# An attention block on one core: late constants among GpSimd's planned work, other PSUM banks for the opening's norms, J1 tiles taken at their addition

## The chip, the core and the metric

The kernel runs on one core of a Trainium2 chip. A core has five engines that run their own instruction streams side by side: TensorE (PE, matrix products into PSUM), VectorE (DVE), ScalarE (ACT, table functions such as the exponential), GpSimd (POOL) and SyncE (SP, which here only issues DMAs). They meet through semaphores. PSUM has eight banks of 128 partitions x 2 KB.

The metric is the time of one execution on the device in microseconds (us), the median over several runs. Before the change it is 359.07 us, the median of 3 runs (359.01 to 359.48).

## The reference

One multi-head attention block: x is 1 x 2048 x 448 in bf16, 16 heads of width 28.

```python
B, S, D = x.shape
H = 16
Dh = D // H
qkv = (x @ wqkv).reshape(B, S, 3, H, Dh).transpose(2, 0, 3, 1, 4)
q, k, v = qkv[0], qkv[1], qkv[2]
scores = jnp.einsum("bhqd,bhkd->bhqk", q, k) * (Dh ** -0.5)
p = softmax(scores, axis=-1)
o = jnp.einsum("bhqk,bhkd->bhqd", p, v)
return o.transpose(0, 2, 1, 3).reshape(B, S, D) @ wo
```

Softmax does not change when one number is taken from all scores of a query. The kernel takes an upper bound on them, made of the norm of the query and the largest norm of the keys.

## The kernel before

**Tiling.** The heads stand in 4 groups of 4 (each padded to 32 rows, so that a group fills 128 partitions), the queries in 4 columns of 512, the keys in 16 tiles of 128. A *set* is one group with one column of queries: 16 sets, in the order ORDER, almost one after the other. Within a set there are 4 x 16 score tiles of 128 keys x 512 queries, one for each head and key tile.

**Two ways to exponentiate.** Most score tiles go in pairs through PSUM tiles a0 and a1 (two banks each) to ScalarE, which takes the exponential of 128 x 1024 numbers at once into a tile `pt` (L1001, `do_exp`). The others go through banks d0 and d1, and now and then m, to VectorE (L1016, `do_a`): it adds a bias, clamps at zero and writes 16-bit integers, whose bits read as bf16 are about 2 to the power of the score. Four such tiles make a *chain*, one tile `I` of 128 x 2048 16-bit integers. To come nearer to the true power, the chain is used three times: as it is, with 43 added to the integers (SHIFT[1], tile J1) and with 85 added (SHIFT[2], tile J2), multiplied with V, V x WT[1] and V x WT[2] (VS or VW in the trace). The additions are VectorE's (L1114, `do_add`; both J1 and J2 appear as J). In sets in the middle, a chain that begins while at least FAR2 = 36 tiles of its set remain doesn't get a J2 from VectorE. There GpSimd issues a DMA that adds a constant tile `shift2` into the chain itself, once the plain chain has been read by PE (`in_place`, L1066, issue at L1074). This is called the in-place line here.

**PE's products.** PE makes scores (L798, into a, d or m), sums the weighted values into bank o (L1176, `do_pv`; four heads side by side, one such group of four matmuls is a *wave*), and in between the projections of later groups (L341 through `mm_proj`, L348 through `quarters`) in bank m. Bank m also takes the output projection. Where PE would idle it multiplies zeros (L830 and `quarters` of `zero`).

**Order.** All of it is a hand-made plan. `plan` runs a model of the five engines in which each operation (class `Op`) has a duration, needs, gives, a priority (a smaller number goes first) and perhaps a PSUM bank to acquire and release; `evt`, `free` and `res` hold the times of events, engines and banks. The plan is made dry with 24 seeds that shake some choices (NSEED), and the shortest is then emitted as instructions. So a change in one rule can alter the order on all engines from there on. `port=True` marks operations that the plan never lets run on GpSimd beside a VectorE operation of the same mark; `after_shared` (L350) adds a semaphore by which a GpSimd operation stays behind the VectorE operation that the plan placed ahead of it. Nothing makes VectorE wait for GpSimd in return. What lies ahead of `plan` (L178 to L261) is not planned: it is a fixed stream on each engine, and the plan only assumes that GpSimd is free from 25.6 us on (L277). GpSimd's fixed stream clears V's tiles (L245, L246), issues 14 DMAs that put offset rows into the QP tiles (L231), then fills `shift2` (L257), copies the identity to fp32 (`identf`, L258, read by the closing transposes at L1428) and makes a small selector (L259, L260).

**The opening.** x's first block is transposed by PE, the other three by DMA (L176). Then come the keys of group 0 in four blocks (`k_first`, L419): product K, its square on ScalarE (L367), the norm of each head's rows by a product with a block of ones (`norm`, L452) into the bank `nbank`, the largest norm on VectorE (`red`, L457, tile kp). After the fourth, `root` (L461, L463) makes the keys' bound. The first query column does the same (`q_job`, `qn_first`, L527 to L550): product, square, norm (L530), root (L534), and the product of both roots, `su` (L539), which the first scores need. Banks are handed on: an operation that acquires a bank waits until its last reader has released it.

**Chains and buffers.** `d_more` starts a chain when `dve_ok` (L840) allows: tile I from six buffers (NCH), tile J1 from five (NJ), both taken at the start of the chain (L892, L895); `j1_free` (L1042) holds back the start of a chain until the J1 of five chains ago has been read. J2 is taken at its addition, from three buffers (L1112, `add_ok`). The rules with FAR and LASTFAR (`far_chain`, `accumulate`) never apply, since a set has 64 tiles and FAR is 99.

**The end.** After the last set, VectorE copies o, PE makes reciprocals' transposes (L1422, L1428), and the output projection of the last column is completed in banks d0, d1, m and one of the a tiles. Parts of it that need only earlier groups (`early_jobs`, `filler`) are placed ahead, as banks come free; those left over stand directly ahead of the last groups (L1437). Two casts on VectorE and two on ScalarE (L1440, L1442) and three DMAs end it.

Of the kernel before, what the change touches and what calls it, by code (L numbers as in the profile page):

```python
# [8 lines left out]
ACT = mybir.ActivationFunctionType  # L9
ALU = mybir.AluOpType  # L10
# [43 lines left out]
def kernel(  # L54
# [7 lines left out]
    nc = tc.nc  # L62
# [31 lines left out]
    NJ = 5  # L94
    FAR = 99
# [5 lines left out]
    LASTFAR = 99  # L101
# [154 lines left out]
    shift2 = const.tile([P, HG * QW], I16, name="shift2")  # L256
    nc.gpsimd.memset(shift2[:].bitcast(I32), SHIFT[2] * 65537)  # L257
    nc.gpsimd.tensor_copy(out=identf[:], in_=ident[:])  # L258
# [5 lines left out]
    def plan(nc, tc, psum, big, wk, dram, seed, dry):  # L264
# [443 lines left out]

        for gg in range(G):
            add("POOL", 0.5, lambda gg=gg: clear_wo(gg), need=[("QA", 0, CL)], gives=[("WZ", gg)], pri=95, port=True)  # L710
# [6 lines left out]
        k_first(1, "a1", "a0", "ACT", "ACT", 3.05, late=("ksq", 0, NQC - 1))  # L717
        k_first(2, "d0", "o", "ACT", "ACT", 3.1, late=("ksq", 0, NQC - 1))
        k_first(3, "d1", "a0", "DVE", "ACT", 3.2, late=("QA", 0, 0))
        q_job(0, 0, "m", QPRI, split=1)  # L720
        qn_first("o", 3.15)
# [47 lines left out]
        chain = {"cur": None, "all": [], "J2": [], "dma": 0.0}  # L769
# [70 lines left out]
        def dve_ok(t, k):  # L840
            if chain["cur"] is None and len(chain["all"]) >= NCH:
                old = chain["all"][-NCH]
                if not j1_free() or not used_up(old, 0) or any(a[0] is old for a in adds) or old["acc"] is None or old["acc"] > t:
                    return False
# [35 lines left out]
        def d_more(s, t, acting):  # L880
            got, taken = [], []
            for b in d_banks(t):
# [183 lines left out]
        def in_place(ch, m):  # L1066
# [3 lines left out]
            if used_up(ch, 0):  # L1070
                evt[("PV0", n)] = (free["PE"], "PE")

            def emit():
                after_shared(nc.gpsimd.dma_start(out=ch["I"][:, w], in_=shift2[:, w], accum_op=ALU.add))  # L1074

            def landed(end):
                at = landing(end)
                for q in range(m):
                    pending.append({"step": ch["steps"][q], "k": 2, "ap": ch["I"][:, q * QW:(q + 1) * QW].bitcast(BF16),
                                    "ready": at, "pt": None, "ch": ch})  # L1080

            add("POOL", 0.88, emit, need=[("line1", n), ("PV0", n)], gives=[("own", n)], pri=9, port=True)
            ops["POOL"][-1].after = landed

        def accumulate(ch, m):
            w = slice(0, m * QW)
            ch["acc"] = None

            def emit():
                after_shared(nc.gpsimd.dma_start(out=ch[1][:, w], in_=ch["I"][:, w], accum_op=ALU.add))  # L1090

            def landed(end):
# [400 lines left out]
```

## Time and profile before

| what | us |
|---|---|
| median of 3 runs | 359.07 |
| span of the profiled execution, first to last instruction | 358.24 |
| time of the profiled execution | 360.29 |
| first exponential begins (L1001) | 17.27 |
| last exponential begins | 348.04 |
| VectorE idle ahead of the closing copies (L1417) | 6.16 |
| POOL busy in the whole span | 115.3 |

The granted clock of TensorE is 1.00 throughout. A group in the page names a line, an engine and an operation, then what is written and read, how often, its busy time and mean duration, and the idle time of the engine just before it with what ended it. A timeline line gives start, duration, engine, line and operation. A matmul or an exponential that is pipelined behind the one ahead of it is recorded with a duration that overlaps, so steps between starts tell more than durations do. Where the page says `shift`, it is `shift2`; buffer numbers are left out.

### The profile page before, as it was taken

Reading aid. Unit: us, or ns where it says so; the run is one execution under the profiler, and the core shown is the slowest. Engines: PE = TensorE matmul, PEld = TensorE weight load, DVE = VectorE, ACT = ScalarE, POOL = GpSimd, SP = SyncE. Lnnn points to the kernel's source line nnn. Section 1 sums busy time; section 2 is a strip of 40 time slices with the busy share of each in tenths; the row PEclk is TensorE's granted clock in tenths of the full one; section 3 lists DMA queues with packets and bytes.
Section 4 is the critical chain, followed back from the end, with each engine's and each line's share of the span. In section 5 each row is a group of like instructions: output and inputs, shape, how many; then the busy total and the mean of one; then the engine's idle time right before and its main releaser. Section 6 shows DMA issues by size and latency. Waiting matters only on the chain.

```text
span 358.2 us, 11057 instructions
## 1 busy us (share of the span) xinstructions
PE 338.0 (94%) x4474; PEld 110.3 (31%) x4474; DVE 329.4 (92%) x616; ACT 338.1 (94%) x370; POOL 115.3 (32%) x164
## 2 busy tenths in 40 slices
PE   8999999999999999999989999988899899999994
PEld 4333233332234332332222222222222322222232
DVE  7789989999999899998999999999999999999933
ACT  2689999999999999999999999999999999999991
POOL 8971252413503043432223535121414131130110
PEclk9999999999999999999999999999999999999999
DMA  9430146551746437094393916464585929395211
GB/s 208 105 97 15 25 95 131 119 112 36 147 98 120 91 61 150 10 191 89 86 186 77 193 34 136 94 139 102 104 165 97 198 62 203 90 185 120 66 33 54
DMA packets 29463, 38.73 MB, mean 108 GB/s; under 512 B 15108, under 2 KB 21092, under 8 KB 29412
## 3 DMA queue, kind: packets, MB, share of 16 engines
q0 software_dynamic: 7648, 26.25, 38.5%
q1 hardware_dynamic: 20516, 11.22, 12.2%
q8 instruction: 35, 0.57, 0.7%
q10 hardware_dynamic: 1248, 0.55, 0.6%
q14 instruction: 16, 0.13, 0.1%
HBM read 6.20 MB, written 1.96 MB: 23 GB/s over the span
## 4 chain that ended last, share of the span: by engine, by line
PE 45%; ACT 37%; issue 7%; DVE 6%; DMA 3%; POOL 0%; SPq 0%; POOLq 0%; ACTq 0%; DVEq 0%
ACT pt L1001 37%; PE a L798 17%; PE o L1176 13%; PE m L341 5%; PE m L348 5%; DVE I L1016 3%; DMA scr<-rec 2%; PE o L696 1%; DVE J L1114 1%; DVE kp L457 1%; DMA rr<-scr 1%; PE d L348 1%; PE d L798 1%; PE a L341 1%; DVE V L612 0%
## 5 line engine op out<-in xcount | busy, mean ns | idle before, releaser
L1001 ACT ACTIVATE pt<-a 128x1024 bf16<-128x1024 f32 x358 | 329.5, 1167 | 3.2 <-PE d L798 1.7
L1016 DVE TENSOR_SCALAR I<-d 128x512 int16<-128x512 f32 x278 | 181.4, 680 | 9.2 <-PE d L798 8.6
L798 PE MATMUL a<-QP,KA 32*128 32x512 bf16 (+1 forms) x708 | 138.2, 380 | 11.3 <-ACT pt L1001 10.3
L1176 PE MATMUL o<-pt,V 128*32 128x512 bf16 x716 | 102.7, 383 | 0.0
L798 PE MATMUL d<-QP,KA 32*128 32x512 bf16 x275 | 95.4, 384 | 0.8 <-DVE I L1016 0.8
L798 PEld LDWEIGHTS <-KA 32*128 32x128 bf16 (+1 forms) x1035 | 48.6, 91 | 145.4 <-issue 143.7
L1074 POOL DMA_DIRECT2D I<-shift x50 | 44.0, 941 | 99.9 <-PE o L1176 28.4
L1114 DVE TENSOR_SCALAR J<-I 128x2048 int16<-128x2048 int16 x104 | 72.9, 709 | 0.7
L1176 PE MATMUL o<-I,V 128*32 128x512 bf16 x308 | 60.0, 385 | 0.0
L1176 PE MATMUL o<-J,VS 128*32 128x512 bf16 x212 | 36.0, 383 | 0.0
L1176 PEld LDWEIGHTS <-V 128*32 128x32 bf16 x1024 | 26.8, 94 | 29.8 <-issue 29.1
L1176 PE MATMUL o<-J,VW 128*32 128x512 bf16 x204 | 31.3, 384 | 0.0
L1228 POOL TENSOR_TENSOR xs<-o_sb,rr 128x512 bf16<-128x512 f32 x12 | 15.9, 1323 | 44.3 <-DMA rr<-scr 21.9
L363 POOL TENSOR_TENSOR sq<-QA 128x512 bf16<-128x512 bf16 x15 | 17.2, 1146 | 23.9 <-DVE QA L503 18.2
L363 POOL TENSOR_TENSOR sq<-KA 128x512 bf16<-128x512 bf16 x12 | 13.4, 1117 | 24.4 <-DVE KA L381 13.8
L1016 DVE TENSOR_SCALAR I<-m 128x512 int16<-128x512 f32 x30 | 20.2, 675 | 0.1
L341 PE MATMUL m<-XT,WRAW 128*32 128x512 bf16 x216 | 18.3, 386 | 0.0
L1228 POOL TENSOR_TENSOR OTL<-o_sb,rr 128x512 bf16<-128x512 f32 x3 | 3.8, 1264 | 34.4 <-DMA rr<-scr 21.7
L1176 PE MATMUL o<-I,VW 128*32 128x512 bf16 x108 | 13.7, 385 | 0.0
L348 PE MATMUL m<-WRAW,XT 128*32 128x112 bf16 (+1 forms) x432 | 13.5, 231 | 0.0
L1176 PEld LDWEIGHTS <-VS 128*32 128x32 bf16 x304 | 10.1, 94 | 9.3 <-issue 8.7
L348 PE MATMUL m<-WO,xs 128*32 128x448 bf16 x156 | 12.7, 358 | 0.0
(133 smaller groups left out, 275.8 us busy)
## 6 DMA issues: line engine op xcount, KB each, us to landing
I<-shift POOLq DMA_DIRECT2D x50, 512.0 KB, 6.0
rr<-scr SPq DMA_DIRECT2D x60, 64.0 KB
QP<-QA SPq DMA_DIRECT2D x60, 28.0 KB
out_dram<-osb SPq DMA_DIRECT2D x12, 112.0 KB
WRAW<-in_wqkv_dram SPq DMA_DIRECT2D x3, 336.0 KB
QP<-su SPq DMA_DIRECT2D x32, 2.0 KB
WO<-in_wo_dram SPq DMA_DIRECT2D x16, 24.5 KB
den<-o_sb SPq DMA_DIRECT2D x15, 8.0 KB
```

Source lines behind the costliest of these rows:

```text
L341: nc.tensor.matmul(out=ps[HP * i:HP * (i + 1), :], lhsT=w[:, cc, h * Dh:h * Dh + HP], rhs=xt(c, cc), start=(cc == 0), stop=(cc == CC - 1), ...
L348: nc.tensor.matmul(out=out[r, :], lhsT=lhsT[:, r], rhs=rhs, start=start, stop=stop, tile_position=(0, HP * i), **k)
L363: after_shared(nc.gpsimd.tensor_tensor(out=t[:], in0=src, in1=src, op=ALU.mult))
L457: nc.vector.reduce_max(out=held["kp"][:, sc:sc + 1], in_=held.pop(nkey), axis=AX.X)
L696: nc.tensor.matmul(out=warm[:], lhsT=zero[:, 0:P], rhs=zero[:], start=True, stop=True)
L798: nc.tensor.matmul(out=out_ap, lhsT=KAt[(g, j // XB)][r, (j % XB) * P:(j % XB + 1) * P], rhs=q[r, :], start=(n == 0), stop=(n == len(terms ...
L1001: nc.scalar.activation(out=pt[:], in_=ps[:], func=ACT.Exp, scale=LN2 / 128.0)
L1016: nc.vector.tensor_scalar(out=dst, in0=pd[:], scalar1=BIAS, scalar2=0.0, op0=ALU.add, op1=ALU.max)
L1074: after_shared(nc.gpsimd.dma_start(out=ch["I"][:, w], in_=shift2[:, w], accum_op=ALU.add))
L1114: cur["shared"] = nc.vector.tensor_scalar(out=r[:, w], in0=ch["I"][:, w], scalar1=float(SHIFT[k]), scalar2=None, op0=ALU.add)
L1176: nc.tensor.matmul(out=o[HP * i:HP * (i + 1), :], lhsT=v_of(e["k"], g, j)[:, HP * i:HP * (i + 1)], rhs=e["ap"], start=(SETMM[key] == 1), s ...
L1228: m = nc.gpsimd.tensor_tensor(out=otile(g, c), in0=st["o_sb"][:], in1=st["rr"][:], op=ALU.mult)
```

## The change

- GpSimd's memset of the shift constant and the copy of the identity leave the fixed stream and become planned operations: the memset is allowed after the evacuation of Q(0,1) (priority 8, ahead of the squares), the copy after the last query column of group 0 is in place (priority 96, behind the clearing of WO). In-place lines need the event "shifts".
- In the opening, the norm of K1 goes to bank o in place of a0, K2's to a0 in place of o, K3's to o in place of a0, and Q's norm to a0 in place of o with priority 2.5 in place of 3.15.
- J1 has four buffers in place of five, and is taken at its addition and not at the chain's start. `dve_ok` no longer asks for it; `add_ok` does.
- A second kind of in-place chain (OWN2), in which the first shift is a DMA too, is added in the code. With OWN2 = 999 it never applies, and only one constant tile is made. The code of FAR and LASTFAR, which never applied, is removed.

```diff
--- before.py
+++ after.py
@@ -91,14 +91,13 @@
     NPT = 10
     NCH = 6
     NCH2 = 3
-    NJ = 5
-    FAR = 99
+    NJ = 4
+    OWN2 = 999
     FAR2 = 36
     ACC_BUSY = 3.0
     FIRST = 1
     RECLAG = 4.0
     OLAST = 4
-    LASTFAR = 99
     AGE = 2.5
     SPLITQ = {1: ([0], [1, 2, 3]), 2: ([0, 1, 2, 3],), 3: ([0, 1, 2, 3],)}
     RR_LAND = 5.0
@@ -253,9 +252,7 @@
     for c in range(NQC):
         offs_rows(c, 1, nc.gpsimd)
 
-    shift2 = const.tile([P, HG * QW], I16, name="shift2")
-    nc.gpsimd.memset(shift2[:].bitcast(I32), SHIFT[2] * 65537)
-    nc.gpsimd.tensor_copy(out=identf[:], in_=ident[:])
+    shifts = {v: const.tile([P, HG * QW], I16, name=f"shift{v}") for v in sorted({SHIFT[1], SHIFT[2], SHIFT[2] - SHIFT[1]} if OWN2 <= S * HG // P else {SHIFT[2]})}
     nc.gpsimd.memset(self_[:], 0.0)
     nc.gpsimd.affine_select(out=self_[:], in_=self_[:], compare_op=ALU.not_equal, fill=1.0, base=-Dh,
                             pattern=[[-HP, HG]], channel_multiplier=1)
@@ -706,6 +703,15 @@
             g, i = divmod(h, HG)
             nc.sync.dma_start(out=WO[HP * i:HP * i + Dh, g, :], in_=wo[h * Dh:(h + 1) * Dh, :])
 
+        def fill_shift(v):
+            after_shared(nc.gpsimd.memset(shifts[v][:].bitcast(I32), v * 65537))
+
+        def copy_ident():
+            after_shared(nc.gpsimd.tensor_copy(out=identf[:], in_=ident[:]))
+
+        for v in shifts:
+            add("POOL", 1.05, lambda v=v: fill_shift(v), need=[("Q", 0, 1)], gives=["shifts"], pri=8, port=True)
+        add("POOL", 0.8, copy_ident, need=[("QA", 0, CL)], gives=["identf"], pri=96, port=True)
         for gg in range(G):
             add("POOL", 0.5, lambda gg=gg: clear_wo(gg), need=[("QA", 0, CL)], gives=[("WZ", gg)], pri=95, port=True)
         for h in range(H):
@@ -714,11 +720,11 @@
             for hf in range(2):
                 xt_first(b, hf, (("d0", "d1"), ("o", "m"))[b][hf])
         k_first(0, "a0", "o", "DVE", "ACT", 1.5)
-        k_first(1, "a1", "a0", "ACT", "ACT", 3.05, late=("ksq", 0, NQC - 1))
-        k_first(2, "d0", "o", "ACT", "ACT", 3.1, late=("ksq", 0, NQC - 1))
-        k_first(3, "d1", "a0", "DVE", "ACT", 3.2, late=("QA", 0, 0))
+        k_first(1, "a1", "o", "ACT", "ACT", 3.05, late=("ksq", 0, NQC - 1))
+        k_first(2, "d0", "a0", "ACT", "ACT", 3.1, late=("ksq", 0, NQC - 1))
+        k_first(3, "d1", "o", "DVE", "ACT", 3.2, late=("QA", 0, 0))
         q_job(0, 0, "m", QPRI, split=1)
-        qn_first("o", 3.15)
+        qn_first("a0", 2.5)
 
         def rows_first():
             for i in range(HG):
@@ -840,7 +846,7 @@
         def dve_ok(t, k):
             if chain["cur"] is None and len(chain["all"]) >= NCH:
                 old = chain["all"][-NCH]
-                if not j1_free() or not used_up(old, 0) or any(a[0] is old for a in adds) or old["acc"] is None or old["acc"] > t:
+                if not used_up(old, 0) or any(a[0] is old for a in adds):
                     return False
                 if old["own"] and not used_up(old, 2):
                     return False
@@ -890,15 +896,12 @@
                 ch = chain["cur"]
                 if ch is None:
                     ch = chain["cur"] = {"I": wk.tile([P, HG * QW], I16, name="I4", bufs=NCH), "s": step[0], "n": 0,
-                                         "got": [0] * NTERM, "m": None, "next": 0, "done": 0, "acc": 0.0, "far": False}
+                                         "got": [0] * NTERM, "m": None, "next": 0, "done": 0}
                     chain["all"].append(ch)
-                    ch[1] = wk.tile([P, HG * QW], I16, name="J1", bufs=NJ)
                     rest = sum(len(q) for q in remain[step[0]])
                     early = FIRST <= step[0] < NSET - 1
                     ch["own"] = early and rest >= FAR2
-                    if early and FAR <= rest < FAR2:
-                        ch["far"] = True
-                        far_chain(ch)
+                    ch["own2"] = early and rest >= OWN2
                 taken.append(ch["next"])
                 ch["next"] = 1 - ch["next"]
                 ch["n"] += 1
@@ -1028,36 +1031,23 @@
         def close(ch, m):
             ch["m"] = m
             ch["at"] = free["DVE"]
-            adds.append([ch, m, 2 if ch["far"] else 1])
+            if not ch["own2"]:
+                adds.append([ch, m, 1])
+                chain["J1"].append(ch)
             if not ch["own"]:
                 chain["J2"].append(ch)
-            if ch["far"]:
-                accumulate(ch, m)
-            elif ch["own"]:
+            if ch["own"]:
                 in_place(ch, m)
 
         def used_up(ch, k):
             return ch["m"] is not None and ch["got"][k] == ch["m"]
 
-        def j1_free():
-            return len(chain["all"]) < NJ or used_up(chain["all"][-NJ], 1)
-
         def add_ok(a):
             if a[2] == 1:
-                return True
+                n = chain["J1"].index(a[0])
+                return n < NJ or used_up(chain["J1"][n - NJ], 1)
             n = chain["J2"].index(a[0])
             return n < NCH2 or used_up(chain["J2"][n - NCH2], 2)
-
-        def far_chain(ch):
-            n = len(chain["all"])
-            fill = SHIFT[1] * 65537
-
-            def emit():
-                m = nc.gpsimd.memset(ch[1][:].bitcast(I32), fill)
-                after_shared(m)
-
-            ch["id"] = n
-            add("POOL", 1.05, emit, gives=[("fill", n)], pri=20, port=True)
 
         def landing(end):
             chain["dma"] = max(chain["dma"], end + ACC_LAND - 1.0 - ACC_BUSY) + ACC_BUSY
@@ -1068,36 +1058,27 @@
             n = ch["id"] = chain["all"].index(ch)
             w = slice(0, m * QW)
             if used_up(ch, 0):
-                evt[("PV0", n)] = (free["PE"], "PE")
-
-            def emit():
-                after_shared(nc.gpsimd.dma_start(out=ch["I"][:, w], in_=shift2[:, w], accum_op=ALU.add))
-
-            def landed(end):
-                at = landing(end)
-                for q in range(m):
-                    pending.append({"step": ch["steps"][q], "k": 2, "ap": ch["I"][:, q * QW:(q + 1) * QW].bitcast(BF16),
-                                    "ready": at, "pt": None, "ch": ch})
-
-            add("POOL", 0.88, emit, need=[("line1", n), ("PV0", n)], gives=[("own", n)], pri=9, port=True)
-            ops["POOL"][-1].after = landed
-
-        def accumulate(ch, m):
...
+                evt[("PV", n, 0)] = (free["PE"], "PE")
+
+            def line(k, need):
+                def emit():
+                    by = SHIFT[k] if not ch["own2"] else SHIFT[k] - SHIFT[k - 1]
+                    after_shared(nc.gpsimd.dma_start(out=ch["I"][:, w], in_=shifts[by][:, w], accum_op=ALU.add))
+
+                def landed(end):
+                    at = landing(end)
+                    for q in range(m):
+                        pending.append({"step": ch["steps"][q], "k": k, "ap": ch["I"][:, q * QW:(q + 1) * QW].bitcast(BF16),
+                                        "ready": at, "pt": None, "ch": ch})
+
+                add("POOL", 0.88, emit, need=need + ["shifts"], gives=[("own", n, k)], pri=9, port=True)
+                ops["POOL"][-1].after = landed
+
+            if ch["own2"]:
+                line(1, [("PV", n, 0)])
+                line(2, [("PV", n, 1)])
+            else:
+                line(2, [("line1", n), ("PV", n, 0)])
 
         def flush():
             ch = chain["cur"]
@@ -1108,8 +1089,7 @@
         def do_add(t):
             ch, m, k = adds[0]
             w = slice(0, m * QW)
-            if k == 2:
-                ch[k] = wk.tile([P, HG * QW], I16, name="J2", bufs=NCH2)
+            ch[k] = wk.tile([P, HG * QW], I16, name=f"J{k}", bufs=NJ if k == 1 else NCH2)
             r = ch[k]
             cur["shared"] = nc.vector.tensor_scalar(out=r[:, w], in0=ch["I"][:, w], scalar1=float(SHIFT[k]), scalar2=None, op0=ALU.add)
             end = port["DVE"] = t + m * QW * 0.00026 + 0.068
```

More of the change, by code (lines that the diff above doesn't have):

```diff
@@ L768, in plan @@
         pts_used = [0]
-        chain = {"cur": None, "all": [], "J2": [], "dma": 0.0}
+        chain = {"cur": None, "all": [], "J1": [], "J2": [], "dma": 0.0}
         a_fifo = []
@@ L1082, in in_place @@
-            add("POOL", 0.88, emit, need=[("line1", n), ("PV0", n)], gives=[("own", n)], pri=9, port=True)
-            ops["POOL"][-1].after = landed
-        def accumulate(ch, m):
[L1086 to L1092, printed above, removed]
-                at = ch["acc"] = landing(end)
-                for n in range(m):
-                    pending.append({"step": ch["steps"][n], "k": 1, "ap": ch[1][:, n * QW:(n + 1) * QW].bitcast(BF16),
-                                    "ready": at, "pt": None, "ch": ch})
-            evt[("I4", ch["id"])] = (free["DVE"], "DVE")
-            add("POOL", 0.88, emit, need=[("fill", ch["id"]), ("I4", ch["id"])], gives=[("acc", ch["id"])], pri=10, port=True)
-            ops["POOL"][-1].after = landed
+                evt[("PV", n, 0)] = (free["PE"], "PE")
@@ L1143, in pv_cands @@
                         out_.append(e)
-            out_.sort(key=lambda e: 0 if not e["ch"] else -1 if e["ch"]["own"] and e["k"] == 0 else
-                      bool((e["ch"]["far"] and e["k"] == 1 or e["ch"]["own"] and e["k"] == 2) and t < e["ready"] + 1.5))
+            out_.sort(key=lambda e: 0 if not e["ch"] else -1 if e["ch"]["own"] and e["k"] == 0 or e["ch"]["own2"] and e["k"] == 1 else
+                      bool(e["ch"]["own"] and e["k"] == 2 and t < e["ready"] + 1.5))
             return out_
@@ L1186, in do_pv @@
                         e["ch"]["got"][e["k"]] += 1
-                        if e["k"] == 0 and e["ch"]["own"] and used_up(e["ch"], 0):
-                            evt[("PV0", e["ch"]["id"])] = (end, "PE")
+                        if e["ch"]["own"] and used_up(e["ch"], e["k"]):
+                            evt[("PV", e["ch"]["id"], e["k"])] = (end, "PE")
             if not any(remain[s]) and outst[s] == 0:
```

## The prediction

> **What bounds the kernel now.** I read the busy shares first, then ScalarE's timeline, then VectorE's beside GpSimd's, and last the end of the chain of waits. The page says that three engines are nearly full, and that each waits for another somewhere:
>
> ```profile
> PE 338.0 (94%) x4474; PEld 110.3 (31%) x4474; DVE 329.4 (92%) x616; ACT 338.1 (94%) x370; POOL 115.3 (32%) x164
> L1001 ACT ACTIVATE pt<-a 128x1024 bf16<-128x1024 f32 x358 | 329.5, 1167 | 3.2 <-PE d L798 1.7
> L798 PE MATMUL a<-QP,KA 32*128 32x512 bf16 (+1 forms) x708 | 138.2, 380 | 11.3 <-ACT pt L1001 10.3
> ```
>
> PE waits 10.3 us for the exponentials (L1001), these wait 3.2 us for PE: ScalarE is the bound, PE close behind. Its timeline gives the long runs, and single entries the step between two starts:
>
> ```profile
> 26.13 136.08 ACT L1001 ACTIVATE pt<-a 128x1024 bf16<-128x1024 f32 x148 [0.89 <-PE d L798]
> 166.46 161.78 ACT L1001 ACTIVATE pt<-a 128x1024 bf16<-128x1024 f32 x176 [0.21 <-PE o L1176]
> ...
> 23.30 1.02 ACT L1001 ACTIVATE pt<-a 128x1024 bf16<-128x1024 f32 x1
> 24.20 1.03 ACT L1001 ACTIVATE pt<-a 128x1024 bf16<-128x1024 f32 x1
> 26.13 1.02 ACT L1001 ACTIVATE pt<-a 128x1024 bf16<-128x1024 f32 x1 [0.89 <-PE d L798]
> ```
>
> An undisturbed step is 24.20 - 23.30 = 0.90 us (0.904 on the mean of such steps); 136.08/148 = 0.919 is the step of a long run. Over all 358 starts, from 17.27 to 348.04, the steps over 0.94 us add up to 6.7 us more than 0.904 each. The largest of all is 24.20 to 26.13: 1.93, so 1.03 us lost at one place. VectorE and GpSimd show why:
>
> ```profile
> 22.30 1.91 DVE L1114 TENSOR_SCALAR J<-I 128x2048 int16<-128x2048 int16 x1
> ...
> 22.68 0.97 POOL L257 MEMSET shift<- 128x1024 int32 x1
> 23.58 0.77 POOL L258 CAST identf<-ident 128x128 f32<-128x128 bf16 x1
> ...
> 24.85 0.37 PE L798 MATMUL d<-QP,KA 32*128 32x512 bf16 x1 [0.81 <-DVE I L1016]
> ```
>
> An addition J<-I (L1114) takes 0.68 at the median of 104. This one takes 1.91 and ends at 24.21, which is 0.56 behind the end of the memset (22.68 + 0.97 = 23.65). Another pair shows the same law:
>
> ```profile
> 137.63 0.88 POOL L1074 DMA_DIRECT2D I<-shift  x1 [1.98 <-PE o L1176]
> 138.24 1.34 POOL L363 TENSOR_TENSOR sq<-KA 128x512 bf16<-128x512 bf16 x1
> 138.91 1.23 DVE L1114 TENSOR_SCALAR J<-I 128x2048 int16<-128x2048 int16 x1
> ```
>
> GpSimd's pass ends at 139.58, the addition at 140.14: 0.56 later again. So an addition cannot proceed beside a GpSimd pass, and VectorE's delay of 1.91 - 0.68 = 1.23 reached ScalarE as 1.03.
>
> **The late constants.** The memset (0.97) and the cast (0.77) leave GpSimd's fixed stream. The instruction order of the changed kernel has the memset directly ahead of the square of Q(0,1), waiting for VectorE's evacuation QA (28.05 to 28.72 in the trace), and the cast behind the four WO memsets. Near 22.3 there remain the DMA issues for QP rows, until 22.68, and two small operations (0.10 and 0.19). If the addition starts freely it ends at 22.98 and the whole 1.03 is gained. If the DMA issue held it until 22.68 and the two small operations until 22.97, it ends at 22.97 + 0.56 = 23.53: 0.55 of 1.23 stays; ScalarE had absorbed 1.23 - 1.03 = 0.20, so 0.35 stays and 0.68 is gained. Two VS copies (L631) ran at 21.18 beside such issues in their usual 0.48, which speaks for the free end: I take 0.95, ends 0.68 and 1.03.
>
> [...]
>
> Where the two go: the memset would run about 28.8 to 29.8 on today's clock, under two evacuations from PSUM (L1016); the next two additions start at 29.84, so it is hidden by a margin of 0.06 us. Without that cover it costs up to 0.97. Behind it stands the square of Q(0,1), which the new order releases only after those two additions, at about 31.1, until 32.1; its reader, the norm of Q(0,1), ran at 32.91. So I cost the delay at nothing. The constant is first read by the in-place line at 47.70, and identf only in the closing transposes (L1428, 351.26): 19 us and far more of cover. The WO memsets now lie between in-place lines; SP's 16 loads behind them serve the output projection, which starts in the last quarter. Nothing.
>
> **The opening's norms.** PE's order changes from norm K0, K2, norm K1, norm Q, K3, norm K2, norm K3 to norm K0, norm Q, K2, norm K1, a filler, K3, norm K2, two fillers, norm K3. Norm Q finds its bank a0 free (K0's evacuation ended at 10.42, Q's square at 10.44) when PE comes to it at 10.72; norm K1, now in bank o, has to wait for the first reduction, which ended at 11.95, before its 12.14. VectorE has the same operations, Q's root one reduction earlier: it fills a gap of 0.6 that stood at 11.95. In the trace norm K2 waited 0.2 us for that root (13.91), which vanishes; but the last reduction began at 14.98, directly behind norm K3 (14.57 + 0.38), and that behind its square (13.83 + 0.69) and K3 itself (12.68). None of these hangs on a norm's bank. K2 no longer follows a filler in its own bank, so it could start at 11.03 (its weights) in place of 11.16. Its data and K3's are transposing DMAs whose landings the views do not show, so the gain is between 0 and 0.13; I take 0.05.
>
> **The J1 buffers and the new order.** The tile J1 is now taken when its addition is placed, four buffers in place of five, and a chain no longer waits for one to start. From about 45 us on the planner's order differs. Counted over the whole kernel: 358 exponentials as before, 308 score tiles on VectorE as before, 106 additions for 104, 48 in-place lines for 50, 56 filler quarters on PE for 72. Two additions cost 2 x 0.70 = 1.4 us on VectorE; between 30 and 330 us it is busy 289 of 300, so I hide them in those 11 us of idle time and price them at 0, upper end 1.4. The fillers are placed where PE has room: 0. Behind 35 us the late steps add up to 4.9 us now; the four largest (0.66, 0.57, 0.50, 0.37) are 2.1 of it. A new order may drop or repeat them: 0, ends -0.9 and +0.9, under half of that sum each way.
>
> **The end.** The chain's last pieces are PE d, then VectorE's two casts:
>
> ```profile
> 353.08 0.36 PE L348 MATMUL a<-WO,xs 128*32 128x448 bf16 x4
> 353.27 0.36 PE L348 MATMUL a<-WO,OTf 128*32 128x448 bf16 x4
> ...
> 353.13 0.62 DVE L1440 CAST pt<-d 128x448 bf16<-128x448 f32 x1 [0.30 <-PE d L348]
> 353.75 0.62 DVE L1440 CAST pt<-a 128x448 bf16<-128x448 f32 x1
> ```
>
> Between PE's last d/m groups and OTf's last group the new order has 12 of the a<-WO,xs quarters for 4. Four ran in 0.19 (353.08 to 353.27), so eight more are 0.39, and the last group ends near 354.02 for 353.63, and its cast, which was waiting for VectorE until 353.75, starts at 354.06: 0.31 later, and with it the last store. I take +0.31, ends 0 and 0.39.
>
> **Sum.** -0.95 - 0.05 + 0 + 0 + 0.31 = -0.69 on the profiled execution, whose time is 360.29: a span of 358.24 and 2.05 around it, which the change doesn't touch. The median of the runs, 359.07, is 1.22 below that time, so only the difference is carried over. A late evacuation of V at 32.55 (a step of 1.18, 0.28 lost) follows the stall and may go with it; I allow 0.08 of it. So -0.77, and 359.07 - 0.77 = 358.3. About 0.2%, 0.7 us, is what a measurement of this kernel can tell from no change, so the forecast lies just beyond it.
>
> **Rivals.** (A) The new order brings more: chains start without waiting for J1 and the planner's clock is no longer 1.2 us wrong on VectorE, so two or three of the four large late steps go. -0.77 - 0.9 gives 357.4. For it: 0.57 at 332 and 0.50 at 327 were a GpSimd product and an in-place line that came late. Against: nothing in the counts removes such places. (B) The gain is given back in the last quarter: counting PE's waves between pairs of score matmuls, what exceeds two waves per step is 4 waves more in the new order outside the closing stage. At 0.216 each that is 0.86, and with -0.77 the time is 359.2, no change. Against: in the trace steps of three waves are mostly absorbed. (C) VectorE becomes the bound: its additions in the middle sets wait for one of the four J1 buffers, and score tiles stand behind them. It decides from the point where these waits use up the idle time that the two further additions need. Then their 1.4 counts in full, with one addition's 0.65 of wait in front: -0.77 + 1.4 + 0.65 = 1.28 over, 360.35. For it: 92% busy, one buffer less. Against: the 11 us of idle time. (D) The change doesn't do what it says: the DMA issues held the addition all along. Then -0.68 + 0.31 - 0.05 = -0.42: 358.65, no measurable change.
>
> **Chances.** Forecast 0.45, A 0.22, B 0.13, C 0.10, D 0.10. The forecast's own range is 357.8 to 358.8, the bounds of the addition and the end with a part of the order's; the bound of 0.2% lies at 358.35, so I count 0.28 of its 0.45 as faster and 0.17 as the same. A is all faster (0.22); B is 0.10 the same and 0.03 slower, since its four waves may come with late steps of their own; C is slower; D is 0.07 the same and 0.03 faster. Together faster 0.53, same 0.34, slower 0.13. The range for 8 in 10 reaches past A's value by 0.2 and past B's by 0.3, and leaves out C: 357.2 to 359.5.
>
> **What would show it.** J<-I near 22.3 at 0.68 us and no step of 1.93 in ScalarE's starts; the memset near 28 with the two additions behind it at their usual length; the first exponential at 17.2 to 17.3; the same 358 at a mean step of 0.918 to 0.920 after 26 us; from the last exponential's start to the end 10.5 for 10.2. I am wrong if the addition at 22.3 is still long, if the memset meets the additions behind it, or if the steps after 45 us lose 1 us more or less than the 4.9 they lose now.

## The result, and the profile after

| | median us | executions |
|---|---|---|
| before | 359.36 (358.79 to 361.11) | 22 |
| changed | 360.26 (359.31 to 363.77) | 22 |

The ratio is 1.0034, 95% interval 1.0017 to 1.0050: the changed kernel is slower by 0.34%, some 1.2 us. The forecast was 358.3, with 357.2 to 359.5 as the range for 8 in 10; the median lies above it.

The two profiled executions tell it the other way round. That of the changed kernel has a span of 357.3 us and took 359.49, 0.8 under its median; that of before had 358.2 and 360.29, about 1 over its own. So the traces are read for places here, and the sums are left to the medians. First the page of the changed kernel, shares and the two costliest groups:

```profile
PE 335.7 (94%) x4456; PEld 109.7 (31%) x4456; DVE 328.9 (92%) x618; ACT 337.9 (95%) x370; POOL 114.4 (32%) x162
L1004 ACT ACTIVATE pt<-a 128x1024 bf16<-128x1024 f32 x358 | 329.3, 1156 | 3.2 <-PE a L804 2.7
L804 PE MATMUL a<-QP,KA 32*128 32x512 bf16 (+1 forms) x708 | 138.0, 381 | 12.0 <-ACT pt L1004 10.9
```

The balance of the engines is as it was; the exponentials (now L1004) still wait 3.2 us for PE. Where they wait is another matter. ScalarE's timeline (start, duration, then the idle time before it and its releaser):

```profile
16.65 1.94 ACT L1004 ACTIVATE pt<-a 128x1024 bf16<-128x1024 f32 x2 [0.75 <-PE a L804]
18.78 66.42 ACT L1004 ACTIVATE pt<-a 128x1024 bf16<-128x1024 f32 x72 [0.19 <-PE d L804]
86.07 12.94 ACT L1004 ACTIVATE pt<-a 128x1024 bf16<-128x1024 f32 x14 [0.86 <-PE a L804]
100.08 63.48 ACT L1004 ACTIVATE pt<-a 128x1024 bf16<-128x1024 f32 x69 [1.07 <-PE a L804]
...
165.83 182.62 ACT L1004 ACTIVATE pt<-a 128x1024 bf16<-128x1024 f32 x199 [0.16 <-PE o L1156]
```

The break at 26.13 is gone, and two new ones stand at 86.07 and 100.08. As steps between starts they are 2.13 (from 83.94) and 2.24 (from 97.84), so 1.23 and 1.34 more than 0.904. All late steps together (what the steps over 0.94 us take beyond 0.904 each) are 6.5 us for 6.7: without the 1.03 at 24.2 before had 5.7, without the two new breaks the changed kernel has 4.0. So in this trace 1.7 us of late steps vanished, and 2.57 us stand in two new places.

The stretch of the moved memset, VectorE and GpSimd:

```profile
21.68 0.69 DVE L1094 TENSOR_SCALAR J<-I 128x2048 int16<-128x2048 int16 x1
...
25.17 0.95 POOL L707 MEMSET shift<- 128x1024 int32 x1 [1.69 <-DVE VS L628]
28.02 1.28 DVE L1094 TENSOR_SCALAR J<-I 128x2048 int16<-128x2048 int16 x2
29.45 1.04 POOL L360 TENSOR_TENSOR sq<-QA 128x512 bf16<-128x512 bf16 x1 [3.33 <-DVE J L1094]
```

The addition J<-I takes 0.69, the memset meets no addition, the two additions at 28.02 have their usual length, and the square of Q(0,1) follows them. The direct part did what was foretold.

The new breaks, both in this trace. At 85 us:

```profile
80.11 0.68 DVE L500 CAST QA<-m 128x512 bf16<-128x512 f32 x1
...
82.71 1.26 POOL L1208 TENSOR_TENSOR xs<-o_sb,rr 128x512 bf16<-128x512 f32 x1 [6.49 <-DMA rr<-scr]
83.95 2.03 POOL L360 TENSOR_TENSOR sq<-QA 128x512 bf16<-128x512 bf16 x2
...
85.03 0.40 PE L345 MATMUL m<-sq,maskK 128*32 128x512 bf16 x4 [1.22 <-POOL sq L360]
```

On GpSimd the squares of the query blocks (1,0) and (1,1), group 1 with the first two query columns, stand behind the product `xs` of the second set (`o_sb` times the reciprocals `rr`), and that waits until 82.71 for the DMA that brings `rr`. Block (1,0) is ready at 80.79 (its cast QA, 80.11 + 0.68), but its square begins only at 83.95, when the product is done. PE's norm of that block (m<-sq,maskK) therefore waits 1.22 us, and PE's score products are behind it. At 98 us (SPq are DMA issues on SyncE):

```profile
80.82 13.38 SPq L505 DMA_DIRECT2D QP<-QA  x12
94.25 2.10 SPq L569 DMA_DIRECT2D QP<-su  x2
...
97.84 0.29 DVE L562 TENSOR_SCALAR su<-z 128x512 int16<-128x512 int16 x1 [1.78 <-DMA QP<-su]
98.79 0.37 PE L804 MATMUL d<-QP,KA 32*128 32x512 bf16 x1 [1.17 <-DVE I L1019]
```

`su`, the bound's row, has one buffer. VectorE wants to write the next one and waits 1.78 us until the DMA of the one before has read it. That DMA was issued at 94.25 only, behind twelve issues QP<-QA in a row of 1.1 us each. Behind VectorE's `su` stand its score tiles, so bank d stays taken and PE waits 1.17.

The same two places in before:

```profile
82.67 0.68 DVE L503 CAST QA<-m 128x512 bf16<-128x512 f32 x1
...
83.16 1.26 POOL L1228 TENSOR_TENSOR xs<-o_sb,rr 128x512 bf16<-128x512 f32 x1 [9.29 <-DMA rr<-scr]
84.39 1.03 POOL L363 TENSOR_TENSOR sq<-QA 128x512 bf16<-128x512 bf16 x1
86.22 1.04 POOL L363 TENSOR_TENSOR sq<-QA 128x512 bf16<-128x512 bf16 x1 [0.80 <-DVE QA L503]
86.48 0.40 PE L348 MATMUL m<-sq,maskK 128*32 128x512 bf16 x4
...
83.39 6.48 SPq L508 DMA_DIRECT2D QP<-QA  x8
90.67 1.22 SPq L572 DMA_DIRECT2D QP<-su  x2
```

There too the product waits for `rr` (until 83.16) and stands ahead of the squares. But block (1,0) is ready only at 83.35, its square ends at 85.42, and the norm comes at 86.48, so nobody waits. And SP issues eight, not twelve, ahead of `su`. The new order has the same sequence on GpSimd, but the block and PE's reader are placed earlier: where nothing holds it the norm starts at 83.90, against 85.14 in before's order without the stall near 24 us (both in runs below).

The closing casts and products:

```profile
352.29 0.74 PE L345 MATMUL a<-WO,xs 128*32 128x448 bf16 x12
...
352.86 0.36 PE L345 MATMUL a<-WO,OTf 128*32 128x448 bf16 x4
353.34 0.62 DVE L1420 CAST pt<-a 128x448 bf16<-128x448 f32 x1 [0.38 <-PE a L345]
```

There are twelve xs quarters for four, and the last cast now waits 0.38 for PE, as foretold.

### The profile page after: what moved, and what is told of

Its sections match the earlier page's. It is cut to its first block, busy times and chain, and to the rows that moved or that the text cites. A ratio compares the mean times of both kernels' runs of the same rounds, so it can differ in the third digit from the quotient of the medians.

```text
span 357.3 us, 11015 instructions
## 1 busy us (share of the span) xinstructions
PE 335.7 (94%) x4456; PEld 109.7 (31%) x4456; DVE 328.9 (92%) x618; ACT 337.9 (95%) x370; POOL 114.4 (32%) x162
## 4 chain that ended last, share of the span: by engine, by line
ACT 41%; PE 22%; issue 6%; DVE 4%; SPq 1%; DMA 1%; DVEq 0%; ACTq 0%
ACT pt L1004 41%; PE a L804 8%; PE o L1156 8%; PE m L338 2%; PE m L345 2%; DVE I L1019 2%; SPq L505 1%; DVE o_sb L1185 1%; DVE J L1094 1%; DMA QP<-su 1%; SPq L569 0%; PE d L804 0%; PE o L345 0%; PE a L345 0%; DVE z L559 0%
## 5 line engine op out<-in xcount | busy, mean ns | idle before, releaser
L1004 ACT ACTIVATE pt<-a 128x1024 bf16<-128x1024 f32 x358 | 329.3, 1156 | 3.2 <-PE a L804 2.7
L804 PE MATMUL d<-QP,KA 32*128 32x512 bf16 (+1 forms) x273 | 95.4, 384 | 1.2 <-DVE I L1019 1.2
L804 PEld LDWEIGHTS <-KA 32*128 32x128 bf16 (+1 forms) x1035 | 47.4, 91 | 145.2 <-issue 143.4
L1156 PEld LDWEIGHTS <-V 128*32 128x32 bf16 x1024 | 28.1, 94 | 30.0 <-issue 28.0
L1156 PE MATMUL o<-J,VW 128*32 128x512 bf16 x224 | 33.8, 383 | 0.0
L1156 PE MATMUL o<-J,VS 128*32 128x512 bf16 x200 | 31.5, 383 | 0.0
L360 POOL TENSOR_TENSOR sq<-QA 128x512 bf16<-128x512 bf16 x15 | 16.2, 1084 | 21.6 <-DVE QA L500 11.6
L1019 DVE TENSOR_SCALAR I<-m 128x512 int16<-128x512 f32 x32 | 21.8, 680 | 0.0
L1156 PEld LDWEIGHTS <-VW 128*32 128x32 bf16 x320 | 10.0, 94 | 8.1 <-issue 7.3
L1156 PE MATMUL o<-I,VS 128*32 128x512 bf16 x96 | 12.3, 386 | 0.0
```

Of the source, the lines that this page charges most:

```text
L360: after_shared(nc.gpsimd.tensor_tensor(out=t[:], in0=src, in1=src, op=ALU.mult))
L804: nc.tensor.matmul(out=out_ap, lhsT=KAt[(g, j // XB)][r, (j % XB) * P:(j % XB + 1) * P], rhs=q[r, :], start=(n == 0), stop=(n == len(terms ...
L1004: nc.scalar.activation(out=pt[:], in_=ps[:], func=ACT.Exp, scale=LN2 / 128.0)
L1019: nc.vector.tensor_scalar(out=dst, in0=pd[:], scalar1=BIAS, scalar2=0.0, op0=ALU.add, op1=ALU.max)
L1156: nc.tensor.matmul(out=o[HP * i:HP * (i + 1), :], lhsT=v_of(e["k"], g, j)[:, HP * i:HP * (i + 1)], rhs=e["ap"], start=(SETMM[key] == 1), s ...
```

## The experiments

Two theories stood against each other: (P) the direct parts gain some 0.8 us and the two new waits, which come with the order from 45 us on, take more than that back; (R) the loss is in the parts themselves: in the norms, in the four J1 buffers, or in the moved constants. The comparisons use before's executions on the same chip.

**The constants moved by hand, in before's order.** Memset and copy leave the fixed stream and stand behind the VS copies of the third block, without a planned operation.

```diff
-    nc.gpsimd.memset(shift2[:].bitcast(I32), SHIFT[2] * 65537)
-    nc.gpsimd.tensor_copy(out=identf[:], in_=ident[:])
...
+                if (g, b, k) == (0, 2, NTERM - 1):
+                    after_shared(nc.gpsimd.memset(shift2[:].bitcast(I32), SHIFT[2] * 65537))
+                    after_shared(nc.gpsimd.tensor_copy(out=identf[:], in_=ident[:]))
```

> The kernel before, with the memset of the shift constant and the copy of the identity taken out of GpSimd's fixed stream and placed by hand behind the third pair of VS copies, without telling the planner: all other instructions keep the order of before. Theory 1 (the constants' move itself gains, and the loss comes from the new order of the planned work, in which two waits for late DMAs and GpSimd stand): about 0.9 to 1.0 us under before, the addition near 22 us back to 0.68, and a spread like that of before. Theory 2 (moving the constants is itself what hurts, by a meeting on GpSimd's and VectorE's ways later): no gain, or slower than before by up to 1 us.

Measured: 359.02 (12 executions) against 359.23 (35), ratio 0.9990 [0.9977, 1.0003]. Both additions took their 0.69 and no late step is left near 24 us, yet the median fell by 0.2 to 0.4 us, not by the 0.9 expected, and the interval takes in no change.

**The constants as planned operations, in before.** Both as in the change, with the need "shifts".

```diff
+        add("POOL", 1.05, fill_shift, need=[("Q", 0, 1)], gives=["shifts"], pri=8, port=True)
+        add("POOL", 0.8, copy_ident, need=[("QA", 0, CL)], gives=["identf"], pri=96, port=True)
```

> The kernel before with the constants among the planned work alone, as the change has it; opening norms and J1 as before. The order behind 45 us is then that of the changed kernel. Theory 1: like the changed kernel, about 0.5 to 1.2 us over before on the median and a wide spread (1 us and more), with GpSimd's squares late at some 84 us and su late at some 97 us. Theory 2 of the opening or of J1 (the norms' new banks or the four J1 buffers make the loss): at or under the time of before, small spread.

Measured: 360.18, 1.0027 [1.0013, 1.0041]. The same two operations cost 0.27% when the planner places them. PE's norm at 85 us waits again, as expected. The late `su` near 97 us, expected too, is not in this trace: `su` is written at 97.62 without a wait. And now something else shows. PE's timeline, then the stretches of one microsecond (after the length come the busy shares of PE, PEld, DVE, ACT and POOL with their instructions, then the granted clock, the DMA share and GB/s):

```profile
85.12 0.40 PE L346 MATMUL m<-sq,maskK 128*32 128x512 bf16 x4 [1.46 <-POOL sq L361]
```

```profile
84.00:85.00 1.00, 0.00 (x0) 0.00 (x0) 0.37 (x1) 1.00 (x2) 1.00 (x2) 1.00 0.12 30
...
87.00:88.00 1.00, 1.00 (x10) 0.10 (x2) 1.00 (x3) 1.00 (x2) 0.00 (x0) 0.50 0.22 55
88.00:89.00 1.00, 1.00 (x10) 0.14 (x8) 1.00 (x3) 0.55 (x2) 0.00 (x0) 0.50 0.01 2
89.00:90.00 1.00, 1.00 (x11) 0.21 (x11) 0.74 (x2) 0.57 (x1) 0.00 (x0) 0.50 0.00 0
```

After PE's gap of 1.46 us its clock is 0.50 from about 87 to 90: ten or eleven matmuls per microsecond, where between 86 and 87 there were 18, and ScalarE busy at 0.55 in the second of these stretches.

**The norms alone, in before.**

```diff
-        k_first(1, "a1", "a0", "ACT", "ACT", 3.05, late=("ksq", 0, NQC - 1))
+        k_first(1, "a1", "o", "ACT", "ACT", 3.05, late=("ksq", 0, NQC - 1))
...
-        qn_first("o", 3.15)
+        qn_first("a0", 2.5)
```

> The kernel before with the opening's norms in their new banks alone; the order differs in the opening only. Theory 1: 0 to 0.2 us under before, the long addition near 22 us still there. The rival in which the norms are the loss: 0.5 to 1 us over before.

Measured: 359.25, 1.0006 [0.9989, 1.0023]: nothing that can be told. The first exponential begins 8.26 behind the first key square in its trace and in that of the changed kernel, 8.38 in before's (17.27 - 8.89): 0.12 gained, where the start of the first square itself moved between 8.13 and 8.89 over the executions. This trace also shows before's fixed stream once more:

```profile
23.61 0.97 POOL L257 MEMSET shift<- 128x1024 int32 x1
...
23.75 1.37 DVE L1114 TENSOR_SCALAR J<-I 128x2048 int16<-128x2048 int16 x1
...
27.61 133.28 ACT L1001 ACTIVATE pt<-a 128x1024 bf16<-128x1024 f32 x145 [0.51 <-PE d L798]
```

Here the memset begins at 23.61 and meets the next addition, not that of 21.4. ScalarE waits 0.51, where it waited 0.89 in the first profile of before; as steps between starts, 0.67 is lost for 1.03.

**Both new waits removed, in the changed kernel.** Two buffers for `su` (the four J1 tiles leave the room), and the product of the second set emitted behind the squares of the query block.

```diff
-                held[("su",) + key] = su = wk.tile([P, QW], BF16, name="su", bufs=1)
+                held[("su",) + key] = su = wk.tile([P, QW], BF16, name="su", bufs=2)
...
+            if key == ("Q", 1, 1) and "late_mul" in held:
+                held.pop("late_mul")()
...
+                if s == 1:
+                    held["late_mul"] = now
+                else:
+                    now()
```

> The changed kernel with su in two buffers in place of one, and with one GpSimd product (the second set's xs) placed behind the square of Q(1,1) in place of ahead of the squares; all else in the order of the changed kernel. Theory 1: the two steps of 2.1 and 2.2 us at some 84 and 98 us go, so that the median falls by 1.5 to 3 us against the changed kernel, to 357.5 to 358.7, and the spread narrows. Theory 3 (fewer fillers on PE, so a lower granted clock in some executions, and no wait in particular): the median stays within 0.5 us of the changed kernel's 360.2, with executions of a clock of 0.995 and less as before.

Measured: 357.87, 0.9962 [0.9945, 0.9978]. This is faster than both kernels, 1.4 us under before. GpSimd, PE, VectorE and ScalarE in its trace:

```profile
83.62 1.04 POOL L360 TENSOR_TENSOR sq<-QA 128x512 bf16<-128x512 bf16 x1 [1.49 <-DVE QA L502]
84.62 1.27 POOL L1211 TENSOR_TENSOR xs<-o_sb,rr 128x512 bf16<-128x512 f32 x1
...
83.90 0.40 PE L345 MATMUL m<-sq,maskK 128*32 128x512 bf16 x4
...
95.41 0.29 DVE L564 TENSOR_SCALAR su<-z 128x512 int16<-128x512 int16 x1
...
18.95 104.92 ACT L1006 ACTIVATE pt<-a 128x1024 bf16<-128x1024 f32 x114 [0.19 <-PE d L806]
```

The norm begins at 83.90 without idle time, `su` without a wait, and ScalarE runs from 18.95 for 104.92 us without a break. All other work keeps the changed kernel's order, PE's fewer zero products (56 quarters for 72) included, so these are not what costs the time.

**One wait at a time.** First only the second `su` buffer, then only the product behind the squares (the two halves of the diff above).

> The changed kernel with su in two buffers alone. Theory 1 (two waits, each with its own price): the step of some 2.2 us near 98 us goes, the late squares near 84 us stay with the low clock that follows them; 0.6 to 1.3 us under the changed kernel, so 359.0 to 359.6, still with executions at a clock of 0.995 and less. If the late squares alone make the loss: no gain, 360.2.

> The changed kernel with the one GpSimd product behind the square of Q(1,1) alone. Theory 1: PE's wait for the square near 84 us goes, and with it most executions at a clock of 0.995 and less; 1.0 to 1.6 us under the changed kernel, so 358.6 to 359.2. The su step near 98 us stays, at up to 1.3. If the su wait alone makes the loss: no gain, 360.2.

Measured: 359.55, 1.0012 [1.0000, 1.0025], and 359.09, 0.9988 [0.9973, 1.0003]. From the changed kernel's 1.0034 the buffer is worth 0.22% (0.8 us) and the product 0.46% (1.65 us), together 0.68%; both at once gave 0.72%, 2.6 us. That is near what the two steps lost in the changed kernel's trace, 1.23 + 1.34 = 2.57. Each of these differences of ratios is uncertain by some 0.2%, so the sum is shown, its closeness to 2.57 is partly luck, and how the sum is split between the two waits is not shown. With the product alone moved, the wait for `su` stayed and was larger in the trace than expected: ScalarE's step at 97.35 lost 2.03, with the clock at 0.50 behind PE's gap of 1.28.

**The two kernels once more**, to see what repeats from one profiled execution to the next.

> The kernel before, once more, to see which addition meets the memset in another execution. If the meeting moves with GpSimd's DMA issues ahead of it: the addition at some 21 to 22 us takes 0.7 and the next one, 2.3 us later, is the long one (1.2 to 1.9), with ScalarE losing 0 to 0.6 in place of 1.03. If the first profile was typical: 1.9 at some 22 us again.

> The changed kernel, once more. Theory 1: the squares' wait near 84 us and the su wait near 98 us are there again, with other lengths; where PE's gap is longer than in the first profile (1.22), the granted clock falls behind it, as in the run with the constants planned alone (gap 1.46, clock 0.50 for 3.3 us).

Measured: 359.65 and 359.73. In the changed kernel both gaps are back (ScalarE idle 0.97 at 85.94 and 1.08 at 99.96). The fall of the clock that was expected behind a gap longer than 1.22 did not come: PE's gap was 1.32 and the clock stayed at 1.00. In before the stall at 22.3 is not back, and the next addition, which was expected to be the long one, is not long either. GpSimd's and VectorE's timelines of before, second profile:

```profile
22.76 0.54 POOL L231 DMA_DIRECT2D QP<-offs  x1 [0.74 <-DMA QP<-offs]
23.30 0.97 POOL L257 MEMSET shift<- 128x1024 int32 x1
...
22.23 0.69 DVE L1114 TENSOR_SCALAR J<-I 128x2048 int16<-128x2048 int16 x1
24.57 0.69 DVE L1114 TENSOR_SCALAR J<-I 128x2048 int16<-128x2048 int16 x1
```

The last DMA issue waited 0.74 us for an earlier one, the memset began at 23.30 and ended at 24.27, just between the two additions. Nothing was lost. In the first profile, the issues ran through to 22.68.

**The copy by hand, in the changed kernel.** The copy of the identity loses its planned operation and is emitted behind the memset.

```diff
         def fill_shift(v):
             after_shared(nc.gpsimd.memset(shifts[v][:].bitcast(I32), v * 65537))
-
-        def copy_ident():
             after_shared(nc.gpsimd.tensor_copy(out=identf[:], in_=ident[:]))
...
-        add("POOL", 0.8, copy_ident, need=[("QA", 0, CL)], gives=["identf"], pri=96, port=True)
```

> The changed kernel, with the copy of the identity no longer an operation of the plan but placed by hand directly behind the memset of the shift constant. The order of all other work is then that of before, with the norms of the change. Theory 1 (the copy as a planned operation redraws the order and so makes the loss; constants and norms themselves gain a little): 0.2 to 0.5 us under before, so 358.6 to 359.0, with a spread like that of before. If the memset as a planned operation or the norms made the loss: 360.2 as the changed kernel.

Measured: 359.04, 0.9996 [0.9983, 1.0010]. VectorE near 22 us and PE near 85 us in its trace:

```profile
22.16 0.69 DVE L1091 TENSOR_SCALAR J<-I 128x2048 int16<-128x2048 int16 x1
...
85.14 0.40 PE L345 MATMUL m<-sq,maskK 128*32 128x512 bf16 x4
```

One planned operation of 0.8 us, far from every critical place, is the whole difference between the old order and the new one. With it gone, the order is before's but for the opening and the constants, the norm of that block stands at 85.14 without a wait, and the slowdown is gone. The direct parts together are then worth 0.04%, within what can be told.

The code says how so small an operation does it. Of its 24 dry plans the kernel emits the one that ends first by its own model. In before that is the plan of seed 5, which ends at 345.37 us on the model's clock, with seed 8 at 345.54. In the changed kernel seed 5's plan ends at 345.93, so seed 8's, at 345.57, is taken; with the copy by hand seed 5 is back at 345.39 and is taken again. Built with seed 8, before has on VectorE, ScalarE, SP and PE the same order as with the planned constants. So the "new order" is one that before already had among its 24 and passed over by 0.17 us of model time. (These ends come from the plans themselves and are not measured on the chip; why the copy lengthens seed 5's plan is not shown.)

**The two cures in before's order**, with J1 taken at its addition (four buffers) for the room.

> The kernel before with J1 taken at its addition from four buffers (which makes room), su in two buffers and the second set's product behind the square of Q(1,1); the order is that of before but for this product. Theory 1 (the two waits belong to the new order): within 0.3 us of before. If both cures help any order: 1 us and more under before, like the changed kernel with both.

Measured: 359.09, 0.9991 [0.9979, 1.0003]. Before doesn't have these waits, and without them nothing is to be cured. So the 1.4 us of the cured version are not the cures' alone but those of the new order, once its two waits are out. Where that order gains them is not shown place by place.

**Five J1 buffers, in the changed kernel**, taken at the chain's start as in before.

```diff
-    NJ = 4
+    NJ = 5
...
+                    ch[1] = wk.tile([P, HG * QW], I16, name="J1", bufs=NJ)
```

> The changed kernel with five J1 buffers, taken at the start of the chain as before; the order of instructions is the same as that of the changed kernel. Theory 1: J1 has no part in it, the time stays at 360.0 to 360.5. If four buffers make VectorE or PE wait: 0.5 us or more under the changed kernel.

Measured: 360.58, 1.0035 [1.0018, 1.0051], the time of the changed kernel. The built instructions stand in the same order with four and with five, so J1 neither holds anything up nor makes the new order.

## Why the prediction was wrong

1. **The late constants, -0.95: the mechanism right, the size wrong.** The law held (the addition ends some 0.55 us behind GpSimd's pass): in the norms' trace the addition ended at 25.12, 0.54 behind the memset's end at 24.58. And the change removed the meeting. But the meeting of 22.30 belonged to one execution. In others the memset begins at 23.3 to 23.6, because a DMA issue ahead of it waits (0.74 to 1.13 us), and it costs 0.67 as a step (the norms' trace) or nothing (the second profile of before). By hand, the move gave 0.1% [-0.03, 0.23], some 0.2 to 0.4 us; that is under the lower end given, 0.68, though the interval reaches to 0.8. The prediction did note that its execution lay 1.22 over the median; it did not ask whether the largest late step of that execution was part of the 1.22.
2. **Where the constants go, nothing: right for the memset, wrong for the copy.** The memset ran at 25.17, not 28.8, because in the built order it waits for the VS copies ahead only; it met no addition either way. The copy's time was hidden, as said. But it is a planned operation, and as such it made the planner take another plan (point 4). That cost was not among the terms.
3. **The opening's norms, -0.05: the gain came to 0.12** (8.38 to 8.26), next to the upper bound of 0.13, and too small for the medians.
4. **"The J1 buffers and the new order", 0 with ends of -0.9 and +0.9: the step that failed.** Its attribution was wrong: the order comes from the copy as a planned operation, which turned the choice from seed 5 to seed 8, not from J1. Its size was wrong on both sides at once. The order with its two waits removed is about 1.2 us better than before's order with the same direct parts (0.9962 against 0.9996), and the waits take 2.6 us (1.0034 against 0.9962), each uncertain by some 0.8 us. The net, +1.4 on the direct parts' 0.9996, lies outside the ends, which were under half of the old order's four largest late steps and had nothing in them for a wait that the old order does not have. Counting operations (358 exponentials, 308 tiles, 106 additions) could not show it. The places themselves were visible in the instruction order: twelve issues QP<-QA for eight ahead of `su`'s DMA, with one buffer, and PE's norm earlier behind a product that was known to wait for `rr` until 83.16.
5. **The end, +0.31: the mechanism right.** SP's last issue comes 6.73 behind the last exponential's start (353.99 - 347.26) for 6.36 (354.40 - 348.04): +0.37. In this execution the last DMA landed faster (3.31 us after its issue for 3.84), and the whole stretch is 10.04 for 10.20.
6. **0.08 for the step at 32.55** hung on point 1 and is too small to be told.

Of the rivals, C's time (360.35) is nearest to what came, but not its mechanism: VectorE does wait for a buffer, but for that of `su` and not of J1, and the other wait is PE's for GpSimd. A was right that fewer late steps remain apart from the two new waits: 4.0 for 5.7 in the first profiles, 5.0 for 6.3 in the second ones. B's give-back in the last quarter isn't there: in the changed kernel's first profile ScalarE runs from 165.83 to its last exponential without a break. D is refuted by the run with the copy by hand: there the addition at 22.16 took 0.69 while GpSimd's DMA issues ran on until 22.95.

Still open is why the changed kernel's executions spread so far (359.31 to 363.77). Seven of the 22 have a mean clock under 0.997 and a median of 361.3, the other fifteen 360.0. But with the planned constants in before the three of low clock are not the longer ones (359.8 against 360.6), so the clock is not shown to be the cause.

## What to carry to other kernels

Where a planner makes the order, a cheap operation added far from the critical path may change everything behind it: read the new order for places where one engine's reader has moved and the slow thing in front of its source (an in-order DMA wait, here that for `rr` until 82.71; a buffer held by a queued transfer, here `su`'s, for which VectorE waited 1.78 us) has not, and price those. Before a loss seen in one execution is entered as a gain, look at a second execution, above all when the first lies over the median. Where the planner picks among plans, look also at which one it picked and by how much: here a margin of 0.17 us by the model decided between orders that differ by more on the chip. And a reordering that came out slower may hold a faster kernel: two local cures turned 1.0034 into 0.9962.

## What the hardware showed beyond that

- TensorE's clock fell to 0.50 for some 3.4 us after a gap of 1.46 us (planned constants, 85.1), and likewise after gaps of 1.47 (second `su` buffer, 85.0) and 1.28 (product behind the squares, 98.4; ScalarE then stood idle for 1.82 until 100.28). It stayed at 1.00 after gaps of 1.32 and 1.18 (second profile of the changed kernel) and of 1.22 and 1.17 (its first profile). So the length of the gap alone doesn't decide, and what does is not shown.
- A DMA issue on GpSimd's queue can itself wait, by the profile for an earlier DMA of that queue (0.74 in the second profile of before, 1.13 in the norms' trace, 0.86 in that of the two cures in before's order), and in the first profile of before none did: the 14 issues ran from 14.69 to 22.68. So the fixed stream behind them had no fixed time: the memset began at 22.68 in the first profile of before, at 23.30 in the second, at 23.38 with the two cures and at 23.61 in the norms' trace, under the same fixed stream.
- What the prediction calls a law, that an addition which meets a GpSimd pass ends some 0.55 us behind it, is in each of these pairs: in the first profile of before 5 of the 104 additions J<-I take over 0.76 us, in that of the changed kernel 5 of 106, and each ends 0.54 to 0.56 us behind a pass that it overlaps. It is 0.55 in the trace of the planned constants (93.30 behind 92.75) and 0.54 in those of the norms (25.12 behind 24.58) and of the two cures in before's order (24.89 behind 24.35). In all of them but that of 22.30, recorded 0.38 ahead of its memset, the pass is recorded as begun first. Two further additions are recorded as begun first and keep nearly their usual length, and there the pass is the longer one: in the second profile of before the selector's last operation, recorded at 24.61, 0.04 behind an addition of 0.69, takes 0.69 where it took 0.19 in the first profile; in the first profile of the changed kernel a memset of WO at 47.55, 0.21 behind an addition of 0.71, takes 1.07 where the next two take 0.81. Why the addition of 22.30 was the longer one all the same is not shown.
